# A filter layer's passages through memory dealt anew: rows kept on the chip for two groups instead of four, GpSimd's subtracts ahead of its sends, direct rows from group 10 on, the fourth inverse tile asked for sooner

## The chip, the cores and the metric

The kernel runs on one core of a Trainium2 chip. The metric is the device time of one execution in microseconds (us), the median of several runs; here three runs of the kernel before gave 1383.17, 1384.69 and 1389.86 us. Lower is better. The profile comes from one more execution, taken by the hardware profiler.

Engines are called PE (TensorE matmul), DVE (VectorE), ACT (ScalarE), POOL (GpSimd) and SP (SyncE, which here only issues DMAs). ACT and POOL can issue DMAs too. "SPq" and the like in the profile are the time in which an engine's instruction stream issues DMAs.

## What is computed

Four layers follow one another on x of 2048 rows by 576 columns: attention, filter, attention, filter, each with a layernorm ahead and a residual added. The change touches the filter alone:

```python
def _B_ref(x, w_r, w_i):
    X = rfft2(x, axes=(-2, -1))
    W = w_r + 1j * w_i
    X = X * W
    return irfft2(X, s=(S, D), axes=(-2, -1))      # S = 2048, D = 576
...
x = x + _A_ref(_layernorm(x), A_wqkv, A_wo)        # 32 heads, causal window of 256
x = x + _B_ref(_layernorm(x), B_w_r, B_w_i)
x = x + _A_ref(_layernorm(x), A_wqkv, A_wo)
x = x + _B_ref(_layernorm(x), B_w_r, B_w_i)
```

## The kernel before, in words

**The filter as matmuls.** The transform along the 2048 rows is split as 128 x 16. Sixteen row groups n2 = 0..15 (each 128 rows, 16 apart) each get a transform of length 128 (`f3`, the `pz` matmuls at L289, then `f4`, L296 to L335); that is the forward stage. Sixteen frequency groups g = 0..15 then each take 8 of the 128 results of every n2, 16 x 8 = 128 rows together, and get the transform of length 16, the weights W and the way back (`g0`, `g1m` with the `p` matmuls L476 and L478, `g2` with the `pq` matmuls L497): the middle stage. Sixteen row groups n2 again close with the inverse transform of length 128 (`ly` L551, `i1` with `pi` L560, `i2`, `i3` with `po` L251) and the transform along the columns. In the first filter layer the column transform stands ahead of the row transform (`f1`, `f2`); in the second layer it has been folded into the attention layer's output, so that its forward stage is shorter.

**Two transposes go through memory.** Between the stages the data has to be regrouped: 8 partitions of each of 16 tiles make one tile of 128 partitions. A forward tile `ye` (128 partitions x 580 floats, 290 KB) is written whole to a DRAM tile `yd[0]` (L326); a middle group g is read back from there (L464, two groups per load, 580 KB; the first such load is split into two of 290 KB). The same happens after the middle stage with tiles `ze`/`eo` and `yd[1]` (stores L534), which the inverse stage reads back one n2 at a time (L554).

**Direct rows.** A transpose that ends with "last tile written, then read back" would leave the next stage waiting, so a few tiles that are needed first are also filled directly, chip memory to chip memory, 8 partitions at a time (18.1 KB each). Forward: from n2 = FD = 11 on, every `ye` sends its 8 partitions of groups 0 and 1 (first layer) or 0 to 3 (second layer) by rows (L321) into the middle stage's tiles; what n2 < 11 contributes comes by a bulk load from `yd[0]` (L335, 88 rows of two groups each; one such load in the first layer, two in the second). Middle to inverse: from g = FG = 11 on, every tile sends its 8 partitions of n2 = 0, 1, 2 by rows (L504) into three inverse tiles; bulk loads (L525) bring groups 0 to 7 at g = 10 and 8 to 10 at g = 13.

**Who sends.** The last `ye` tiles are dealt to three engines, for each issue takes its engine about 0.5 to 0.65 us. Second layer: n2 up to 12 and 15 by SP, n2 = 13 by POOL, n2 = 14 by ACT. First layer: n2 = 14 by POOL, all else by SP. In the second layer n2 = 12, 13, 14 have half of `f4`'s arithmetic on POOL (`P.tensor_sub`, L303; ACT's copy of the matmul's result is L293), and n2 = 15 has both halves on DVE (L309, L310).

**Order and waits.** Nothing here is scheduled by a tool: each engine runs its instructions in the order in which the code emits them (`pipe` and the written-out lists call the functions above), and a waiting instruction holds up all behind it on the same engine. DMAs that SP and ACT issue share eight completion semaphores, called DMAHW0 to DMAHW7 and here lanes, handed out in turn over both in an order fixed when the program is built, in which ACT's DMAs stand among SP's. A DMA waits until the one before it on its lane has landed. POOL's DMAs have eight lanes of their own, DMASW0 to DMASW7. So at most eight SP and ACT DMAs are in flight, and an SP DMA can be held by an ACT DMA that has not even been issued.

**Fill-ins.** At the end of the second layer's forward stage 34 matmuls without use (`warm(34)`, L341) keep PE going while the last rows travel, and 36 ahead of its inverse stage. In the first layer useful matmuls (`wo`, L251) stand at these places.

**Residual rows.** `ld` (L164) brings x back for the inverse stage, from g = 11 and 13 on; `i1` adds to it (L562) and the first layer writes it out (L564).

The line that deals the last tiles is the one that names cannot say:

```python
eng = nc.sync if n2 < NT - 3 or n2 == NT - 1 else P if first is (n2 == NT - 2) else nc.sync if first else nc.scalar
```

## Time and profile before

| what | value |
|---|---|
| median of three runs | 1384.69 us (1383.17 to 1389.86) |
| the profiled execution's own time | 1384.23 us |
| its span (first to last instruction) | 1382.3 us |
| granted PE clock, mean | 0.996 |
| PE busy | 1341.2 us, 97% of the span |
| DVE, ACT, POOL busy | 65%, 57%, 47% |
| second layer: forward stage's last `pz`, first `p`, first `pq` | 1259.1, 1272.43, 1278.18 us |
| first layer: first `p`, first `pq` | 604.43, 608.61 us |
| first `pi`: first layer, second layer | 649.30, 1319.14 us |

How to read the views. The *timeline* prints start, duration, engine and line, operation, tile written <- tile read, shape, count, and in square brackets the idle time ahead with what ended it. In a row of SPq, POOL DMA or ACTq the duration is that of the issue, with waits between the joined issues; landing comes later. The *waits* view gives, for an engine's line, the total of its waits, how many, and the longest. The *chain* follows the work that ended last, back from the end, each piece with start and duration; a piece "DMA" is a transfer from issue to landing. The *windows* view has, for each stretch, its length, each engine's busy time in the order PE, PE weight load, DVE, ACT, POOL, then the granted clock (PEclk), the share of the DMA engines' time, and GB/s.

### The profile page before, as it was taken

The page shows a single profiled execution, that of the slowest core. Times are in us where ns is not written, and L with a number is a line of the kernel's source. Part 1 is how long each engine was busy: PE and PEld are TensorE (multiplying, and loading weights), DVE is VectorE, ACT ScalarE, POOL GpSimd, SP SyncE. Part 2 cuts the span into 40 slices and gives each one's busy share as a digit, 9 for nine tenths or more (in the row PEclk, how much of TensorE's full clock was granted, in tenths as well). Part 3 has the DMA queues.
Part 4 walks back from the last instruction along what each step waited for, and adds up shares of the span by engine and source line. Part 5 has one row for each costly group of instructions (what it writes and reads, how often), then busy time and mean ns, then how long its engine had stood idle before and what let it go on. Part 6 is the DMA issues. An engine that isn't in the chain of part 4 may idle for free.

```text
span 1382.3 us, 33597 instructions
## 1 busy us (share of the span) xinstructions
PE 1341.2 (97%) x11356; PEld 998.3 (72%) x11356; DVE 892.7 (65%) x3046; ACT 786.9 (57%) x1978; POOL 646.4 (47%) x1152
## 2 busy tenths in 40 slices
PE   9999999999999999999999999999999999997998
PEld 8985666666665699975899965666666655996588
DVE  5417777877778266566663157787777783563845
ACT  5522777777778544443355316677777778562223
POOL 2257554555547433476221394455545457111821
PEclk9999999999999999999999999999999999999999
DMA  6756665655556457678863467556554565597874
GB/s 202 210 164 185 204 187 174 184 164 164 150 147 181 109 168 238 214 241 272 262 211 73 125 195 220 162 170 165 167 155 143 155 173 153 163 375 216 268 230 159
DMA packets 202478, 259.09 MB, mean 187 GB/s; under 512 B 104589, under 2 KB 109965, under 8 KB 201797
## 3 DMA queue, kind: packets, MB, share of 16 engines
q1 hardware_dynamic: 191573, 235.70, 56.8%
q10 hardware_dynamic: 7856, 15.33, 3.2%
q0 software_dynamic: 2880, 5.93, 1.6%
q8 instruction: 91, 1.49, 0.5%
q14 instruction: 78, 0.64, 0.1%
HBM read 155.98 MB, written 101.01 MB: 186 GB/s over the span
## 4 chain that ended last, share of the span: by engine, by line
PE 81%; POOL 4%; DMA 4%; ACT 4%; DVE 3%; issue 3%; SPq 1%; ACTq 0%; DVEq 0%; POOLq 0%
PE pj L1079 15%; PE S L1136 12%; PE U L1193 11%; PE vps L972 8%; PE ops L767 7%; PE E L1173 5%; PE po L251 4%; PE p L476 2%; PE pf L251 2%; PE tpo L1207 2%; PE pi L560 2%; PE pq L497 2%; ACT P L1174 2%; POOL qs L1227 2%; POOL ks L1226 2%
## 5 line engine op out<-in xcount | busy, mean ns | idle before, releaser
L1138 DVE CUSTOM_DVE_ANT_0 jk<-S,mask 128x384 bf16<-128x384 f32 (+2 forms) x1024 | 490.6, 529 | 112.9 <-PE E L1173 59.3
L1174 ACT ACTIVATE P<-E 128x384 f32<-128x384 f32 (+2 forms) x1024 | 409.5, 476 | 122.9 <-PE E L1173 101.6
L1176 POOL TENSOR_SCALAR_AFFINE_SELECT P<-P 128x512 f32<-128x512 f32 x256 | 163.2, 638 | 280.1 <-ACT P L1174 259.8
L1136 PE MATMUL S<-ks,qs 63*128 63x384 f32 (+2 forms) x1024 | 269.1, 371 | 0.6 <-DVE m L1138 0.4
L1173 PE MATMUL E<-qs,ks 64*128 64x384 f32 (+2 forms) x1024 | 222.4, 372 | 3.5 <-ACT P L1174 1.9
L1136 PEld LDWEIGHTS S<-ks,qs 63*128 63x128 f32 x1024 | 140.6, 185 | 105.3 <-DVE m L1138 72.3
L1193 PE MATMUL U<-P,vq 128*19 128x128 f32 (+1 forms) x3840 | 187.8, 328 | 1.0 <-ACT us L1198 1.0
L1079 PE MATMUL pj<-xh,wqh 128*128 128x512 f32 x360 | 156.1, 434 | 1.4 <-DVE sg L1094 1.0
L1193 PEld LDWEIGHTS U<-P,vq 128*19 128x19 f32 x3840 | 95.6, 98 | 77.5 <-issue 21.8
L1179 POOL TENSOR_SCALAR_AFFINE_SELECT P<-P 128x512 f32<-128x512 f32 x224 | 143.0, 638 | 0.0
L1079 PE MATMUL pj<-xh,wql 128*128 128x512 f32 x360 | 125.8, 423 | 2.4 <-POOL wql L657 2.4
L1173 PEld LDWEIGHTS E<-qs,ks 64*128 64x128 f32 x1024 | 114.3, 185 | 18.2 <-ACT P L1174 8.2
L1079 PE MATMUL pj<-xl,wqh 128*128 128x512 f32 x288 | 122.0, 424 | 0.0
L767 PE MATMUL ops<-oroom 128*128 128x290 f32 (+1 forms) x812 | 115.4, 298 | 0.2
L767 PEld LDWEIGHTS ops<-oroom 128*128 128x128 f32 x812 | 110.3, 189 | 0.7 <-DVE ofree L790 0.7
L1079 PEld LDWEIGHTS pj<-xh,wqh 128*128 128x128 f32 x360 | 67.8, 188 | 32.1 <-issue 10.6
L1094 DVE TENSOR_TENSOR sg<-pj,sg 128x512 fp32r<-128x512 f32 x72 | 49.5, 687 | 56.2 <-ACT sg L1091 56.2
L1138 DVE DVE_READ_ACCUMULATOR2_ANT m<- 128x1 f32 x1024 | 85.0, 83 | 0.0
L1091 ACT CAST sg<-pj 128x512 fp32r<-128x512 f32 x72 | 42.2, 586 | 73.0 <-PE pj L1079 63.1
L1079 PEld LDWEIGHTS pj<-xh,wql 128*128 128x128 f32 x360 | 64.8, 190 | 23.5 <-issue 10.7
L243 ACT CAST et<-tp 128x512 fp32r<-128x512 f32 x53 | 31.2, 589 | 74.1 <-PE tp L239 71.9
L972 PE MATMUL vps<-wvh,xh 128*128 128x288 f32 x320 | 71.4, 304 | 0.1
(225 smaller groups left out, 2304.5 us busy)
## 6 DMA issues: line engine op xcount, KB each, us to landing
qk_d<-sg SPq DMA_DIRECT2D x56, 512.0 KB
qs<-qk_d SPq DMA_DIRECT2D x384, 72.0 KB
ks<-qk_d SPq DMA_DIRECT2D x348, 72.0 KB
v_d<-vt SPq DMA_DIRECT2D x32, 304.0 KB
vq<-v_d SPq DMA_DIRECT2D x16, 608.0 KB
wt<-in_w SPq DMA_DIRECT2D x16, 580.0 KB
ofree<-x SPq DMA_DIRECT2D x16, 580.0 KB
x<-ofree SPq DMA_DIRECT2D x32, 290.0 KB
```

The lines of the kernel that those rows point to most:

```text
L251: T.matmul(ps[:, c, 0:NF], tail[r] if si == 4 else hl_(si), dcs[b // 2][r, b % 2], start=mi == si == 0, stop=si == 4)
L767: self.nc.tensor.matmul(self.ps[u][n][:, 0:self.n], x, self.w[p][:, (2 * wk + n) * self.n:(2 * wk + n + 1) * self.n], start=first and i == ...
L972: T.matmul(ps[:, n, 0:288], xT(xk, c), w[:, wk, n * 288:(n + 1) * 288], start=i == 0, stop=i == len(ks) - 1)
L1079: T.matmul(box["ps"].rearrange("r (n p) -> r n p", n=NT) if second else box["ps"], w[:, wk], x, start=s == 0, stop=s == len(ks) - 1)
L1094: V.tensor_sub(rest[:, 1], by, rest[:, 0].bitcast(F32))
L1136: T.matmul(ps[:, 0:N], q[b:b + 63, pair, i * 128:i * 128 + 128], k[b:b + 63, pair, lo:hi], start=True, stop=True)
L1138: V.tensor_tensor_reduce(out=jk[:, 0:N], in0=ps[:, 0:N], in1=mask[:, 384 - N:384], scale=1.0, scalar=-3e38, op0=ALU.add, op1=ALU.max, accu ...
L1173: T.matmul(ps[:, 0:nq], k[b:b + 64, pair, j * 128:j * 128 + 128], q[b:b + 64, pair, j * 128:j * 128 + nq], start=True, stop=True)
L1174: A.activation(p[:, hl_, 0:nq], ps[:, 0:nq], AF.Exp, scale=SC)
L1176: P.affine_select(out=p[:, :, 0:128], in_=p[:, :, 0:128], pattern=[[0, 4], [1, 128]], compare_op=ALU.is_ge, fill=0.0, base=0, channel_mult ...
L1179: P.affine_select(out=p[:, :, 256:384], in_=p[:, :, 256:384], pattern=[[0, 4], [-1, 128]], compare_op=ALU.is_gt, fill=0.0, base=0, channel ...
L1193: T.matmul(U[32 * h:32 * h + 19, (q0 % 4) * 128:(q0 % 4) * 128 + 128 * (q1 - q0)], vts[n][:, j, h], pt[n, j][:, h, (q0 - j) * 128:(q1 - j) ...
```

## The change

Four things change in the filter layer, in both filter layers unless said otherwise. Line numbers after the change differ; the row send is then L316, the store of a whole `ye` L319, the bulk load L313, the load of groups L474, the rows of the second passage L514, their bulk loads L541, the stores L546, the loads of inverse tiles L569.

1. **Forward rows for groups 0 and 1 only.** The second layer's groups 2 and 3 come back from DRAM like the others; the split load is that of g = 2 in both layers. The one bulk load is issued ahead of n2 = 11's rows.
2. **Second layer, n2 = 13, 14, 15.** POOL first makes its subtracts for 12, 13 and 14; all sends follow after the arithmetic of n2 = 15: rows of 13 by POOL, row 14 for group 0 by SP and for group 1 by POOL, rows of 15 by SP, then the stores: 13 by POOL, 15 by SP, 14 by POOL. ACT sends nothing here any more.
3. **Direct rows of the second passage from g = 10 on** (FG = 10). Bulk loads: groups 0 to 7 at g = 9, ahead of that group's own store, and groups 8 and 9 at g = 11. SP sends the rows to n2 = 0, to n2 = 1 up to g = 12, and one to n2 = 2; ACT those of g = 13 and 15 to n2 = 1; POOL that of g = 14 to n2 = 1, then the store of g = 14, then the other rows to n2 = 2. The held store of g = 13 comes ahead of POOL's last two rows. `ld` is called at g = 10 and 12.
4. **The fourth inverse tile** (n2 = 3), which has no direct rows, is asked for at the start of the inverse stage instead of three steps later.

```diff
@@ -137,7 +137,7 @@
 
     yd = [dram.tile([16, 16, 8, 2 * NF], F32, name=f"yd{j}") for j in range(2)]
     OPEN = *range(2, 17, 2), 17
-    FD, FG, SH = 11, 11, 192
+    FD, FG, SH = 11, 10, 192
     near, NY = 3, 3 if first else 4
     with ExitStack() as stack:
         banks, inner = ExitStack(), ExitStack()
@@ -304,35 +304,45 @@
             else:
                 both = ip.tile([128, 2, NF], F32, tag="both", name=f"half{n2}", bufs=2)
                 A.copy(both[:, 0], pz[:, 1, 0:NF])
-                if not first and n2 == NT - 1:
-                    hs[n2 - 1]["send"]()
                 V.tensor_add(ye[:, 0], pz[:, 0, 0:NF], both[:, 0])
                 V.tensor_sub(ye[:, 1], pz[:, 0, 0:NF], both[:, 0])
             yef = ye.rearrange("p j f -> p (j f)")
             pre(n2)
-            wide = 1 if first else 2
             if n2 == FD:
-                for k in range(wide):
-                    y_tile(k)
-            eng = nc.sync if n2 < NT - 3 or n2 == NT - 1 else P if first is (n2 == NT - 2) else nc.sync if first else nc.scalar
-
-            def rows(lo, hi):
-                for g in range(lo, hi):
-                    eng.dma_start(ys[g][8 * n2:8 * n2 + 8].rearrange("p c f -> p (c f)"), yef[8 * g:8 * g + 8])
-
-            def send():
-                if n2 >= FD:
-                    rows(0, 2 if n2 == NT - 1 else 2 * wide)
+                y_tile(0)
+                nc.sync.dma_start(pairs[0].rearrange("p (a f) -> p a f", a=2)[0:8 * FD], yd[0][0:2, 0:FD].rearrange("a n i f -> (n i) a f"))
+
+            def row(eng, g):
+                eng.dma_start(ys[g][8 * n2:8 * n2 + 8].rearrange("p c f -> p (c f)"), yef[8 * g:8 * g + 8])
+
+            def whole(eng):
                 eng.dma_start(yd[0][:, n2], yef)
-                if n2 == NT - 1:
-                    rows(2, 2 * wide)
-            if eng is nc.scalar:
-                h["send"] = send
+
+            if n2 < FD:
+                whole(nc.sync)
+            elif first:
+                e = P if n2 == NT - 2 else nc.sync
+                for g in range(2):
+                    row(e, g)
+                whole(e)
+            elif n2 < NT - 3:
+                for g in range(2):
+                    row(nc.sync, g)
+                whole(nc.sync)
             else:
-                send()
-            if n2 == FD:
-                for k in range(wide):
-                    nc.sync.dma_start(pairs[k].rearrange("p (a f) -> p a f", a=2)[0:8 * FD], yd[0][2 * k:2 * k + 2, 0:FD].rearrange("a n i f -> (n i) a f"))
+                h["rows"] = [lambda e, g=g: row(e, g) for g in range(2)]
+                h["whole"] = whole
+            if not first and n2 == NT - 1:
+                a, b, c = hs[n2 - 2:]
+                a["rows"][0](P)
+                a["rows"][1](P)
+                b["rows"][0](nc.sync)
+                b["rows"][1](P)
+                c["rows"][0](nc.sync)
+                c["rows"][1](nc.sync)
+                a["whole"](P)
+                c["whole"](nc.sync)
+                b["whole"](P)
 
         def warm(n):
 
@@ -460,7 +470,7 @@
         def g0(g, h):
             if g % 2 == 0 and g not in ys:
                 y = y_tile(g // 2).rearrange("p a c f -> p a (c f)")
-                for a in ((0, 1), (1, 2)) if g == (2 if first else 4) else ((0, 2),):
+                for a in ((0, 1), (1, 2)) if g == 2 else ((0, 2),):
                     nc.sync.dma_start(y[:, a[0]:a[1]], yd[0][g + a[0]:g + a[1]].rearrange("a n i f -> (n i) a f"))
             h["y"] = ys[g]
 
@@ -476,8 +486,8 @@
                     T.matmul(ps[64 * j:64 * j + 64, c, 0:NF], fc[:, g, j, c], h["y"][:, j], start=True, stop=g > 0)
                     if g == 0:
                         T.matmul(ps[64 * j:64 * j + 64, c, 0:NF], fc[:, 16, j, c], h["y"][:, 1 - j], start=False, stop=True)
-            if g in (11, 13):
-                ld(g - 11)
+            if g in (10, 12):
+                ld(g - 10)
             w = wt[g]
             p1 = tws[g % 2]
             p2 = wp.tile([128, 2, NF], F32, tag="tc", name=f"p2_{g}", bufs=3)
@@ -509,26 +519,28 @@
                 V.tensor_sub(ye[:, 1], pq[:, 0, 0:NF], both[:, 1])
                 if first:
                     w1(3)
-                for n2 in range(2):
-                    rows(nc.sync, n2, 15)
+                rows(nc.sync, 0, 15)
+                for k in (13, 15):
+                    rows(nc.scalar, 1, k)
+                held.pop()()
                 for k in (14, 15):
                     rows(P, 2, k)
-                held.pop()()
             else:
                 A.copy(both, pq[:, :, 0:NF])
                 P.tensor_sub(ye[:, 1, 0:SH], both[:, 0, 0:SH], both[:, 1, 0:SH])
                 V.tensor_add(ye[:, 0], pq[:, 0, 0:NF], both[:, 1])
                 V.tensor_sub(ye[:, 1, SH:NF], pq[:, 0, SH:NF], both[:, 1, SH:NF])
-            if g in (FG - 1, FG + 2):
+            if FG <= g < 15:
+                for n2 in range(1 if g > 12 else 2):
+                    rows(nc.sync, n2, g)
+            if g == 12:
+                rows(nc.sync, 2, FG)
+            if g in (FG - 1, FG + 1):
                 lo, hi = (0, 8) if g < FG else (8, FG)
                 for n2 in range(near):
                     nc.sync.dma_start(yis[n2][8 * lo:8 * hi].rearrange("p c f -> p (c f)"), yd[1][n2, lo:hi].rearrange("g i f -> (g i) f"))
             if g == 14:
-                for k in range(FG, 14):
-                    rows(P, 2, k)
-            if FG <= g < 15:
-                for n2 in range(2):
-                    rows(P if g == 14 and n2 else nc.sync, n2, g)
+                rows(P, 1, 14)
 
             def store():
                 (P if g == 14 else nc.scalar if g < 13 and (g < 8 or g % 2 == 0) else nc.sync).dma_start(yd[1][:, g], yef)
@@ -536,6 +548,9 @@
                 held.append(store)
             else:
                 store()
+            if g == 14:
+                for k in range(FG + 1, 14):
+                    rows(P, 2, k)
 
         zs, held = {}, []
         pipe(16, [(10, g2), (7, g1m), (2, gw), (0, g0)])
@@ -549,9 +564,9 @@
             next(nxt)
 
         def ly(n2, h):
-            y = h["y"] = yis[n2 % 4]
-            if n2 >= near:
-                nc.sync.dma_start(y.rearrange("p c f -> p (c f)"), yd[1][n2].rearrange("g i f -> (g i) f"))
+            h["y"] = yis[n2 % 4]
+            for k in (near,) if n2 == 0 else (n2,) if n2 > near else ():
+                nc.sync.dma_start(yis[k % 4].rearrange("p c f -> p (c f)"), yd[1][k].rearrange("g i f -> (g i) f"))
 
         def i1(n2, h):
             pi = pp.tile([128, 2, 512], F32, tag="mm", name=f"pi{n2}", bufs=3)
```

**On SP, end of the second layer's forward stage, before.** The names: `ye_19786` is n2 = 12, `ye_19825` is n2 = 15; `ofree` is the memory of the middle stage's tiles; the brackets hold the semaphores waited for.

```order
L321 DMA ofree<-ye_19786 8x580 [waits DMAHW7_49,DVE_49,Pool_49]
L321 DMA ofree<-ye_19786 8x580 [waits DMAHW1_49]
L321 DMA ofree<-ye_19786 8x580 [waits DMAHW2_49]
L321 DMA ofree<-ye_19786 8x580 [waits DMAHW3_49]
L326 DMA yd_18874<-ye_19786 16x8x580 [waits DMAHW4_49]
L321 DMA ofree<-ye_19825 8x580 [waits DMAHW5_49,DVE_49]
L321 DMA ofree<-ye_19825 8x580 [waits DMAHW6_49]
L326 DMA yd_18874<-ye_19825 16x8x580 [waits DMAHW7_49]
L321 DMA ofree<-ye_19825 8x580 [waits DMAHW0_49]
L321 DMA ofree<-ye_19825 8x580 [waits DMAHW1_49]
L464 DMA ofree<-yd_18874 128x580 [waits DMAHW4_49,DMAHW2_49,DMAHW7_49,DMASW2_49,Activation_49]
```

On ACT at the same place, where `ye_19813` is n2 = 14:

```order
L321 DMA ofree<-ye_19813 8x580 [waits DMAHW1_49,DMAHW6_49,DVE_49,Pool_49]
L321 DMA ofree<-ye_19813 8x580 [waits DMAHW3_49,DMAHW2_49]
L321 DMA ofree<-ye_19813 8x580 [waits DMAHW4_49]
L321 DMA ofree<-ye_19813 8x580 [waits DMAHW6_49]
L326 DMA yd_18874<-ye_19813 16x8x580 [waits DMAHW0_49]
```

**After,** on SP, from n2 = 12 (`ye_19786`) over n2 = 14 (`ye_19806`) and 15 (`ye_19818`) to the first load of the middle stage:

```order
L316 DMA ofree<-ye_19786 8x580 [waits DVE_49,Pool_49]
L316 DMA ofree<-ye_19786 8x580 [waits DMAHW4_49]
L319 DMA yd_18877<-ye_19786 16x8x580 [waits DMAHW5_49]
L316 DMA ofree<-ye_19806 8x580 [waits DMAHW6_49,DVE_49,Pool_49]
L316 DMA ofree<-ye_19818 8x580 [waits DMAHW7_49,DVE_49]
L316 DMA ofree<-ye_19818 8x580 [waits DMAHW0_49]
L319 DMA yd_18877<-ye_19818 16x8x580 [waits DMAHW1_49]
L474 DMA ofree<-yd_18877 128x580 [waits DMAHW1_49,DMAHW2_49,DMASW2_49,DMAHW5_49,DMASW1_49,PE_49]
L474 DMA ofree<-yd_18877 128x580 [waits DMAHW3_49,PE_49]
```

Before, SP's second row of n2 = 12 and ACT's first row of n2 = 14 have the same lane, DMAHW1, in which ACT's comes first; ACT's five took lanes 1, 3, 4, 6 and 0. After, ACT's are gone, SP has two rows of n2 = 12 and one of n2 = 14, and the store of n2 = 15 stands behind both its rows; the loads of group 2 now stand where those of group 4 stood.

**On POOL at the same place.** Before (`ye_19803` is n2 = 13, `ye_19813` is n2 = 14):

```order
L303 TENSOR_TENSOR ye_19786<-half_19774 128x290 [waits DMAHW0_49,DMAHW3_49,DVE_49,Activation_49]
L303 TENSOR_TENSOR ye_19803<-half_19804 128x290 [waits DMAHW4_49,DVE_49,Activation_49]
L321 DMA ofree<-ye_19803 8x580 [waits DMAHW2_49,DMAHW6_49,DVE_49,Pool_49]
L321 DMA ofree<-ye_19803 8x580 [waits DMAHW7_49,DMAHW2_49]
L321 DMA ofree<-ye_19803 8x580 [waits PE_49] x2
L326 DMA yd_18874<-ye_19803 16x8x580
L303 TENSOR_TENSOR ye_19813<-half_19814 128x290 [waits DMAHW0_49,Activation_49]
```

After (`ye_19801` is n2 = 13, `ye_19806` is n2 = 14):

```order
L303 TENSOR_TENSOR ye_19786<-half_19774 128x290 [waits DMAHW3_49,DMAHW6_49,DVE_49,Activation_49]
L303 TENSOR_TENSOR ye_19801<-half_19802 128x290 [waits DMAHW7_49,DVE_49,Activation_49]
L303 TENSOR_TENSOR ye_19806<-half_19807 128x290 [waits DMAHW3_49,DMAHW1_49,Activation_49]
L316 DMA ofree<-ye_19801 8x580 [waits DMAHW1_49,DMAHW5_49,DVE_49,Pool_49]
L316 DMA ofree<-ye_19801 8x580 [waits DMAHW5_49,DMAHW2_49]
L316 DMA ofree<-ye_19806 8x580 [waits DVE_49,Pool_49]
L319 DMA yd_18877<-ye_19801 16x8x580
L319 DMA yd_18877<-ye_19806 16x8x580
```

The subtract of n2 = 14 moves from behind the five sends of n2 = 13 to ahead of all sends; two rows of n2 = 13 fall away, one row and the store of n2 = 14 are new.

**On SP, start of the first layer's inverse stage.** Before, from the last store of the middle stage (`ze_10158`, g = 15) on:

```order
L534 DMA yd_8102<-ze_10158 16x8x580 [waits DMAHW4_49]
L164 DMA ofree<-x_59 128x1160 [waits DMAHW5_49,PE_49]
L564 DMA x_60<-ofree 128x580 [waits DMAHW6_49,DVE_49]
L164 DMA ofree<-x_59 128x1160 [waits DMAHW7_49,PE_49]
L554 DMA ofree<-yd_8102 128x580 [waits DMAHW3_49,DMAHW4_49,DMAHW0_49,DMASW1_49]
```

After (`ze_10160` is g = 15):

```order
L546 DMA yd_8102<-ze_10160 16x8x580 [waits DMAHW7_49]
L569 DMA ofree<-yd_8102 128x580 [waits DMAHW6_49,DMAHW7_49,DMAHW0_49,DMASW6_49]
L164 DMA ofree<-x_59 128x1160 [waits DMAHW1_49,PE_49]
L579 DMA x_60<-ofree 128x580 [waits DMAHW2_49,DVE_49]
L164 DMA ofree<-x_59 128x1160 [waits DMAHW3_49,PE_49]
```

The load of inverse tile n2 = 3 moves up past two loads of x and one store of x.

## The prediction

> **What bounds the kernel now.** I read the page first: what share PE has, and whether the chain that ended last runs over PE.
>
> ```profile
> PE 1341.2 (97%) x11356; PEld 998.3 (72%) x11356; DVE 892.7 (65%) x3046; ACT 786.9 (57%) x1978; POOL 646.4 (47%) x1152
> PE 81%; POOL 4%; DMA 4%; ACT 4%; DVE 3%; issue 3%; SPq 1%; ACTq 0%; DVEq 0%; POOLq 0%
> ```
>
> PE is busy for 1341.2 of 1382.3 us. The change leaves PE's matmuls as they are, so it can win only PE's idle time, or lose by adding some. The waits view of PE says where the filter layers leave it idle.
>
> ```profile
> PE p L476 <- DMA ofree<-ye: 8.7, 1, 8.7
> PE pi L560 <- issue: 1.9, 1, 1.9
> PE pi L560 <- DMA ofree<-ze: 1.8, 1, 1.8
> PE pi L560 <- DMA ofree<-yd: 1.1, 1, 1.1
> ```
>
> One wait of 8.7 us for rows and three of 1 to 2 us in the inverse stages are all that the change can reach: 13.5 us. The timeline says which layer the long one is in, and why it is there.
>
> ```profile
> 1258.28 0.80 POOL L303 TENSOR_TENSOR ye<-half 128x290 f32<-128x290 f32 x1 [1.15 <-ACT half L293]
> 1258.96 4.80 PE L341 MATMUL warm<-dc 128*128 128x290 f32 x34
> 1259.27 9.63 SPq L321 DMA_DIRECT2D ofree<-ye  x4
> 1259.49 2.09 POOL L321 DMA_DIRECT2D ofree<-ye  x4 [0.41 <-DVE ye L302]
> 1260.01 0.45 DVE L310 TENSOR_TENSOR ye<-pz,half 128x290 f32<-128x290 f32 x1
> 1261.57 0.55 POOL L326 DMA_DIRECT2D yd<-ye  x1
> 1262.14 0.72 POOL L303 TENSOR_TENSOR ye<-half 128x290 f32<-128x290 f32 x1
> 1262.88 2.78 ACTq L321 DMA_DIRECT2D ofree<-ye  x4
> 1269.62 1.30 SPq L321 DMA_DIRECT2D ofree<-ye  x2
> 1272.43 1.24 PE L476 MATMUL p<-ofree,fc 128*64 128x290 f32 x4 [8.66 <-DMA ofree<-ye]
> ```
>
> It is the second layer. SP needs 9.63 us for the four rows of n2 = 12, of which the waits view of SP puts 7.0 on one landing:
>
> ```profile
> SPq L321 <- DMA ofree<-ye: 7.0, 1, 7.0
> 1262.88 4.01 DMA ofree<-ye
> 1269.62 2.47 DMA ofree<-ye
> 1278.18 2.15 PE pq L497 x8
> ```
>
> The order rows of SP and ACT name it: SP's second row of n2 = 12 has lane 1 behind ACT's first row of n2 = 14. In the chain (the last three rows) that row is issued at 1262.88 and lands 4.01 later, at 1266.89; SP goes on there. ACT's row could not go sooner, since POOL subtracted for n2 = 14 at 1262.14 only, behind five sends of 1259.49 to 1262.12. So the data of n2 = 15, complete at 1260.46 (DVE, 1260.01 + 0.45), is sent at 1269.62, its second row lands for the `p` of group 0 at 1272.43, and the first `pq` starts at 1278.18. A second price hangs on that idle time, in the windows view:
>
> ```profile
> 1264.00:1272.40 8.40, 0.00 (x0) 0.01 (x1) 0.00 (x0) 0.00 (x0) 0.00 (x0) 0.79 0.44 113
> 1272.40:1276.20 3.80, 3.77 (x18) 2.31 (x20) 0.00 (x0) 0.00 (x0) 0.00 (x0) 0.56 0.55 149
> 1276.20:1312.00 35.80, 35.80 (x249) 19.16 (x245) 30.24 (x60) 9.59 (x15) 28.57 (x46) 1.00 0.86 277
> ```
>
> After 8.4 us of idleness the granted clock is 0.56, and group 0 takes 3.80 us. From 1276.2 PE is full to 1312.
>
> **Second layer, forward tail.** ACT's five DMAs leave the lanes, and POOL subtracts before it sends. The subtract of n2 = 14 ends at about 1259.8 (1258.28 + 0.80 + 0.72). The rows of n2 = 12 are two instead of four, 0.65 each. Three rows remain on SP after them: n2 = 14 to group 0 at 1259.8, n2 = 15 at 1260.5 and 1261.15 (not before 1260.46), then the store of n2 = 15 at 1261.8. POOL issues three rows of about 0.52 (2.09 for four) from 1259.8, then its stores at 1261.35 and 1261.9. With 2.47 to landing, the row of n2 = 15 is there at 1263.6. `warm(34)` ends at 1263.76, so group 0 starts at about **1263.8** and the wait of 8.7 us is gone.
>
> What is late next is group 2: it now comes through memory. Its load waits for the stores of n2 = 13, 14, 15. The nearest rows for these landings, the first two from the DMA issues (second and first layer's tail: KB, us to landing), the rest from the first layer, which already runs that way:
>
> ```profile
> yd<-ye POOLq DMA_DIRECT2D x1, 290.0 KB, 5.1
> yd<-ye POOLq DMA_DIRECT2D x1, 290.0 KB, 3.0
> 603.70 8.60 SPq L464 DMA_DIRECT2D ofree<-yd  x6
> 604.50 0.65 PE p L476 x4
> 606.66 1.96 PE p L476 x16
> 608.61 2.15 PE pq L497 x8
> 652.76 6.75 DMA ofree<-yd
> ```
>
> There the load of group 2 was asked at 603.7 and PE went through groups 1 and 2 from 606.66 to 608.61 without a gap, so the load (290 KB) took at most 3.9 us (group 2's half of 1.96 us began at about 607.6); the worst load of 290 KB in a filter layer is the 6.75. At a full clock group 0 takes 2.16 us (604.50 to 606.66) and group 1 0.98. Here group 0 ends at about 1266.0 and group 1 at 1266.95. POOL's last store, issued at 1261.9, lands 3.0 to 5.1 later: 1264.9 to 1267.0. The load takes 3.9 (I keep up to 6.75 for the range). With 3.0 and 3.9 group 2 starts at 1268.8 after an idle 1.85 us, and `pq` at about **1269.5**, with 2.75 as the price of a load in the faster case down to 1268.6. Before it was 1278.18: a gain of **8.6**. Bounds: 5.1 and 6.75 put group 2 at 1273.75 and `pq` at 1274.7, a gain of 3.5; a free landing of all (`pq` as soon as the product of group 0 allows, 608.61 − 604.50 = 4.1 after 1263.8, or 1268.0) gives 10.2.
>
> Two things can hold this. The row of n2 = 14 has the lane of the bulk load, issued now at about 1252.3, when the store of n2 = 10 has landed; even with 7.06 us, the largest piece of the chain that is a load (in the fence below), it lands at 1259.4, ahead of 1259.8: nothing. And later loads are asked as much sooner as group 2 is, so they keep their lead over PE's 2.3 us a group: nothing.
>
> **The Trainium skill speaks against the dealing.** "DMA: Bandwidth & Descriptors", section "Issuing engines are not separate DMA queues", says that DMAs started from several engines run on the same 16 DMA engines, and that spreading them saves only issue time. By that rule alone the three stores and the load are 1.16 MB one after another, whoever sends them; at the 277 GB/s of the full window this is 4.2 us from 1261.4, an estimate that puts group 2 at 1265.6, ahead of PE, so the rule would take nothing from this step. The trace agrees with the rule in kind (POOL's store took 5.1 us beside other transfers, 3.0 without), but what cost 7 us was a lane, not a DMA engine.
>
> **Second layer, inverse start.**
>
> ```profile
> 1305.42 7.06 DMA ofree<-x
> 1312.28 5.06 PE L341 MATMUL warm<-dc 128*128 128x290 f32 x36
> 1313.25 0.45 DVE L509 TENSOR_TENSOR ze<-pq,both 128x290 f32<-128x290 f32 x1
> 1315.49 3.52 DMA ofree<-ze
> 1319.14 2.20 PE L560 MATMUL pi<-ofree,ga 128*128 128x290 f32 x8 [1.80 <-DMA ofree<-ze]
> ```
>
> The last tile is complete at 1313.70, but SP sends its row to n2 = 0 at 1315.49, behind rows of g = 13 and 14. After, SP has one row each of g = 13, 14 and 15 here instead of two, two, of which one by POOL, and two: it issues the last at 1314.1 to 1314.8, and it lands by 1316.6 (with 2.47) to 1318.3 (with 3.52). `warm(36)` ends at 1317.34. `pi` starts at 1317.4 to 1318.3 instead of 1319.14: 0.8 to 1.75, I take **1.5**. ACT's two rows to n2 = 1 follow its last copy, with nothing behind them that is wanted soon; POOL's rows to n2 = 2 come behind two stores now, about 1 us later, but `pi` of n2 = 2 comes over 3 us after the first (the chain has it at 1322.56). The `ld` calls, one group sooner, fall into a stretch in which PE is full: nothing, unless loads then come late (bounded by the 1.0 below).
>
> **First layer, inverse start.**
>
> ```profile
> 648.41 0.54 SPq L164 DMA_DIRECT2D ofree<-x  x1
> 649.30 2.19 PE L560 MATMUL pi<-ofree,ga 128*128 128x290 f32 x8 [1.90 <-issue]
> 649.38 0.59 ACT L243 CAST et<-tp 128x512 fp32r<-128x512 f32 x1 [1.96 <-DMA ofree<-ze]
> 652.76 0.34 SPq L554 DMA_DIRECT2D ofree<-yd  x1
> 659.55 1.25 PE L560 MATMUL pi<-ofree,ga 128*128 128x290 f32 x4 [1.10 <-DMA ofree<-yd]
> ```
>
> The fourth tile's load moves from behind two loads and a store of x to the place of 648.41, where it must wait for the last stores (some 2 us), so 650 to 651, 2 or more before 652.76. Its 6.75 may grow by the transfers that it now runs beside, but it needs to come only 1.1 earlier: the wait of **1.1** goes. The loads of x that it passes are each 0.35 to 0.54 later. The first `pi` could start sooner, as in the second layer, but ACT's cast at 649.38 waits for the same landings and the `wo` matmuls behind the first `pi` wait for it; I give this nothing, with 0 to 1.6 for the two together, and −1.0 if POOL's later rows to n2 = 2 hold it.
>
> The forward tail of the first layer keeps its two rows per tile, and `wo` matmuls cover it until `p` at 604.50: the bulk load's new place costs nothing while they do, at most the few tenths by which its rows follow later.
>
> **Sum,** against the profiled execution's own 1384.23 us (span 1382.3, 1.9 outside; 0.46 under the median of the three runs): 8.6 + 1.5 + 1.1 = 11.2, so **1373.0**.
>
> **Rivals.**
>
> *Congested landings.* Store and load of group 2 take 5.1 and 5 to 6.75 us: `pq` starts at 1272.9 to 1274.7. PE then idles 5 to 6.8 us between groups 1 and 2. A stage gain of 3.5 to 5.3 and 2.6 from the rest give **1376.3 to 1378.1**. For it: POOL's store did take 5.1 here. Against: two bulk loads stood ahead of it, of which one is left, sent 3.6 us sooner.
>
> *The inverse starts give nothing* (1.5 and 1.1 fall away, because the rows of g = 15 land behind stores as at 1315.49, or because ACT's rows share lanes with SP's): **1374.5 to 1375.6**.
>
> *The trip through memory becomes the bound, on the slower side.* If store and load each take 7.06, as the load of x did, group 2 comes at 1261.9 + 14.1 = 1276.0. PE has then been idle for 9 us, longer than the 8.4 after which group 0 took 3.80 us for 2.16. Groups 2, 3 and the first two `pq` at a clock of 0.56 lose about 2 us; the first full `pq` is 1.5 us later than before, and with the inverse starts unchanged: **1385.7**. It decides from group 2 later than 1276.2 on. Against: no store of 290 KB took more than 5.1. "TensorE: Matmul & The Clock Gate" of the Trainium skill, Part 1, puts the drop to half clock after an idle window of about 3.4 us; the trace agrees in kind (0.79 over the idle window, 0.56 behind it), and by it the congested rival would pay 1 to 2 us too and come to 1377 to 1380.
>
> *It doesn't free SP:* another lane or POOL's sends hold the rows of n2 = 15 as long as before. Then only the 2.6 of the rest remain: **1381.6**. The order rows speak against it.
>
> **Chances.** Forecast 0.61 (1371.3 to 1374.5), inverse starts give nothing 0.13, congested landings 0.18, SP not freed 0.04, slower side 0.04. The range 1370.5 to 1378.5 leaves out the last two and a little at the ends. 0.5%, about what a measurement of this kernel can tell from no change, is 6.9 us: faster is below 1377.8. Forecast, inverse case and some 0.11 of the congested one lie there: 0.84; within, 0.13; slower beyond 0.5% is a part of the slower side: 0.03.
>
> **What would show it.** Right: no SP wait of 7 us at the rows of n2 = 12; both rows of n2 = 15 issued by 1262; `p` within 0.3 us of the end of `warm(34)`, and group 0 in 2.2 us; a PE wait of 1 to 3 us at the load of group 2; `pq` 8 to 9 us sooner; `pi` of the second layer waiting under 1 us; no wait at the first layer's fourth `pi`. Wrong: PE waiting 5 us or more for group 2, a granted clock below 1 behind it, or a landing of n2 = 14's store that ends later than 1267.

## The result and the profile after

The changed kernel takes 1387.64 us (median of 22 runs, 1383.39 to 1392.41) against 1383.61 us before (22 runs): ratio **1.0028**, 95% interval 1.0019 to 1.0038. It is slower by about 4 us; forecast were 1373.0 us and a range up to 1378.5. The profiled execution took 1388.67 us with a span of 1387.0 (before: 1384.23 and 1382.3), so the two profiles differ as the medians do, by 4.7 and 4.0 us.

PE's busy time, in a line of the page, has grown by 4.6 us with the same number of matmuls; the mean granted clock of the profiled execution is 0.993 instead of 0.996.

```profile
PE 1345.8 (97%) x11356; PEld 1003.0 (72%) x11356; DVE 892.3 (64%) x3046; ACT 786.5 (57%) x1978; POOL 644.9 (46%) x1152
```

PE's waits in the changed kernel (total, times, longest), in the same view as before:

```profile
PE wo L251 <- DVE et L245: 5.4, 2, 3.0
PE pi L575 <- DMA ofree<-ze: 3.9, 1, 3.9
...
PE wo L251 <- ACT et L243: 2.1, 1, 2.1
PE p L486 <- DMA ofree<-ye: 2.1, 1, 2.1
```

The wait of 8.7 us for rows is down to 2.1; forecast was none. In front of `wo` matmuls, which belong to the first layer's inverse start, PE waits 7.5 us, and the second layer's first `pi` waits 3.9 instead of 1.8 us. Before, the view had for `wo` only

```profile
PE wo L251 <- ACT et L243: 0.7, 1, 0.7
```

To see which stretch gives and which takes, three of them are followed through all kernels below. **A** runs from the start of `warm(34)` to the start of the second `pq` (second layer, forward to middle). **B** runs in the first layer, and **C** in the second, from the start of the last 24 `pq` matmuls (groups 13 to 15) to the start of `pi` of n2 = 4, where the inverse stage has found its pace. Each is the difference of two starts of PE rows in the timeline. For B of the changed kernel these are:

```profile
638.43 3.27 PE L507 MATMUL pq<-uv,m 64*128 64x290 f32 x24
651.27 3.13 PE L575 MATMUL pi<-ofree,ga 128*128 128x290 f32 x8
662.19 1.81 PE L575 MATMUL pi<-ofree,ga 128*128 128x290 f32 x4
666.66 1.14 PE L575 MATMUL pi<-ofree,ga 128*128 128x290 f32 x4
670.18 1.14 PE L575 MATMUL pi<-ofree,ga 128*128 128x290 f32 x4
```

The first `pi` row holds n2 = 0 and 1, the others one n2 each, so B is 670.18 − 638.43 = 31.75 us. Before it was 663.17 − 639.51 = 23.66.

| stretch | before | changed | difference | forecast |
|---|---|---|---|---|
| A, second layer's forward tail | 22.43 | 15.80 | −6.6 | −8.6 |
| B, first layer's inverse start | 23.66 | 31.75 | **+8.1** | −1.1 |
| C, second layer's inverse start | 21.68 | 24.55 | +2.9 | −1.5 |
| sum | | | +4.3 | −11.2 |

The sum accounts for 4.3 of the 4.7 us between the spans. So the gain came, if smaller, and the first layer's inverse start gave it all back. The timeline of the changed kernel there:

```profile
641.64 0.53 ACTq L546 DMA_DIRECT2D yd<-eo  x1
642.26 1.19 ACT L529 COPY both<-pq 128x580 f32<-128x580 f32 x2 [4.14 <-PE pq L507]
642.82 1.99 SPq L514 DMA_DIRECT2D ofree<-eo  x3
646.50 0.53 POOL L530 TENSOR_TENSOR eo<-both 128x192 f32<-128x192 f32 x1 [2.99 <-DMA ofree<-eo]
647.77 0.62 SPq L514 DMA_DIRECT2D ofree<-ze  x1
655.67 0.59 ACT L243 CAST et<-tp 128x512 fp32r<-128x512 f32 x1 [4.79 <-DMA ofree<-eo]
657.37 2.78 PE L251 MATMUL wo<-dc,et 128*128 128x290 f32 x10 [2.97 <-DVE et L245]
```

Two things stand out. ACT stood 4.14 us in front of its copies, behind its store of group 12. And GpSimd's subtract for group 14 (646.50) waited 2.99 us for a *direct row* to land. Group 14 writes into an `eo` tile, of which the first layer has two in turn here (`eos[2 + g // 2 % 2]`): group 14's is that of group 10. Direct rows from group 10 on read that tile, and the last of them, to n2 = 2, is sent by SP at group 12, as the third in the row at 642.82. Before, group 10 had no direct rows. Everything of group 14 comes later by that: SP's last row goes out at 647.77, 9.3 us after the last 24 `pq` began (before: 645.70 and 646.38, so 6.2 and 6.9 us), and a cast that reuses the tiles' memory waits for the last rows until 655.67. The windows view shows what idleness then costs (clock in the third column from the right):

```profile
645.90:648.38 2.48, 0.05 (x1) 0.00 (x1) 1.96 (x5) 0.00 (x0) 1.35 (x3) 0.62 0.08 15
648.38:651.20 2.82, 2.82 (x12) 2.80 (x13) 0.00 (x0) 0.64 (x1) 2.76 (x6) 0.50 0.66 162
651.20:654.40 3.20, 3.20 (x10) 2.04 (x8) 0.00 (x0) 0.00 (x0) 0.00 (x0) 0.67 0.68 181
654.40:657.40 3.00, 0.03 (x1) 0.04 (x1) 0.78 (x2) 0.86 (x2) 0.00 (x0) 0.89 0.42 107
657.40:662.00 4.60, 4.60 (x20) 4.58 (x21) 1.37 (x4) 0.64 (x1) 1.37 (x6) 0.50 0.96 295
```

In 16 us PE works 10.6 at a clock of 0.50 to 0.67.

### The profile page after: what moved, and what is told of

It is laid out like the page before. It is cut to its first block, busy times and chain, and to the rows that moved or that the text cites. A ratio compares the mean times of both kernels' runs of the same rounds, so it can differ in the third digit from the quotient of the medians.

```text
span 1387.0 us, 33579 instructions
## 1 busy us (share of the span) xinstructions
PE 1345.8 (97%) x11356; PEld 1003.0 (72%) x11356; DVE 892.3 (64%) x3046; ACT 786.5 (57%) x1978; POOL 644.9 (46%) x1152
## 4 chain that ended last, share of the span: by engine, by line
PE 81%; DMA 6%; ACT 4%; POOL 3%; DVE 3%; issue 2%; SPq 1%; ACTq 0%; DVEq 0%; POOLq 0%
PE pj L1094 17%; PE S L1151 11%; PE U L1208 10%; PE vps L987 8%; PE ops L782 7%; PE E L1188 5%; PE po L251 4%; PE pf L251 2%; PE p L486 2%; PE pi L575 2%; PE tpo L1222 2%; PE pq L507 2%; ACT P L1189 2%; PE pz L289 1%; DMA qs<-mt 1%
## 5 line engine op out<-in xcount | busy, mean ns | idle before, releaser
L1094 PEld LDWEIGHTS pj<-xh,wqh 128*128 128x128 f32 x360 | 67.7, 188 | 32.6 <-issue 10.5
```

The lines of the kernel that those rows point to most:

```text
L1094: T.matmul(box["ps"].rearrange("r (n p) -> r n p", n=NT) if second else box["ps"], w[:, wk], x, start=s == 0, stop=s == len(ks) - 1)
```

## The experiments

My theory after this reading: part 3 of the change (direct rows from group 10 on) loses what part 2 wins, by the buffer of group 14. The first rival: the lanes, held by the x loads that part 3 asks one group sooner (ACT's 4.14 us). Each kernel was run with 6 to 12 timed runs beside the kernel before; ratios are to the kernel before, with 95% intervals, and "the changed kernel" is always the one of the result.

A, B and C come from one profiled execution of each kernel. How far they scatter can be seen where the code of a stretch is the same. A is 15.66 to 18.40 us in the nine kernels that have the changed forward stage as it is (changed, e1, e4, e5, e6, e8, e9, e12, e15); B is 22.61 to 24.41 and C 20.52 to 22.65 in the four that have the inverse start of e8 (e8, e10, e13, e14). So a difference of under 2 us in B or C, or under 3 in A, shows nothing by itself.

### The parts alone: e1_forward, e2_passage, e3_tile

e1 is the kernel before with parts 1 and 2, e2 with part 3, e3 with part 4; the diffs are those pieces of the change.

> The kernel before with parts 1 and 2 of the change alone (forward rows for two groups, GpSimd's subtracts ahead of its sends, no ACT sends). My theory: this part keeps what the trace of the changed kernel shows of it (the stretch from the last pz to the first pq of the second layer was 6.7 us shorter), and the loss comes from part 3. So 6 to 7 us faster than before, ratio 0.995 to 0.996. Rival: the forward tail gives less by itself, since part of the 6.7 us is only the later start of that stretch (other transfers have drained): 2 to 4 us, ratio 0.997 to 0.999.

> The kernel before with part 3 alone (direct rows from group 10 on, bulk loads at 9 and 11, rows dealt anew, x asked one group sooner). My theory: the whole loss is here, 8 us in the first layer's inverse start and 2 to 3 in the second's, so 9 to 11 us slower than before, ratio 1.0065 to 1.008. Rival: the loss needs part 4 beside it (the fourth tile's load waits for the last stores on SP, and everything of SP stands behind it): then part 3 alone costs 3 us or less.

> The kernel before with part 4 alone (fourth inverse tile asked for ahead of the x loads). Forecast of the prediction: the 1.1 us wait at the first layer's fourth pi goes, ratio 0.999. Rival: the load waits for the last stores and holds the x loads and x stores behind it on SP by 2 to 4 us; pi of the fourth tile then gains nothing, and the time is the same or up to 2 us longer, ratio 1.000 to 1.0015.

| kernel | median us | ratio | A | B | C |
|---|---|---|---|---|---|
| before (profile) | | 1 | 22.43 | 23.66 | 21.68 |
| e1_forward | 1376.17 | 0.9961 (0.9946 to 0.9976) | 16.71 | 24.02 | 21.28 |
| e2_passage | 1395.39 | 1.0095 (1.0079 to 1.0111) | 22.60 | 34.46 | 23.97 |
| e3_tile | 1381.93 | 0.9994 (0.998 to 1.0009) | 22.69 | 24.35 | 21.11 |

Parts 1 and 2 give 5 to 6 us by themselves; part 3 alone costs 13 us, more than the 9 to 11 expected, and needs no part 4; part 4 makes no difference that these runs can tell. The three ratios multiplied give 1.005, more than the change's 1.0028: in company part 3 costs some 3 us less than alone, which these runs don't explain.

### The x loads: e4_ld, e9_xpool

```diff
-            if g in (10, 12):
-                ld(g - 10)
+            if g in (11, 13):
+                ld(g - 11)
```

> The changed kernel with the two x loads back at groups 11 and 13. Theory of the lane: the 580 KB load of x, asked one group sooner, takes 7.3 us and has the lane that ACT's store of group 12 needs; ACT stands 4 us in front of the copies of groups 13 to 15. With the loads back ACT's wait goes and 4 to 7 us of the loss in the two inverse starts, so 1380 to 1383, ratio to before 0.996 to 0.999. Theory of the buffer: the tile of group 14 waits in the first layer for the direct rows of group 10 (3.0 us on POOL), and the rows behind GpSimd's store are late whatever the lanes do: then the gain is under 2 us, ratio to before 1.001 to 1.003.

e9 leaves the loads where the change put them, on another queue:

```diff
-                nc.sync.dma_start(x, xfv[:, n2:n2 + 2])
+                (P if n2 < 4 else nc.sync).dma_start(x, xfv[:, n2:n2 + 2])
```

> The changed kernel with the first two loads of x (580 KB each, ahead of the inverse stage) issued by GpSimd, so that they use no lane of SP and ACT. Theory of the lane: ACT's store of group 12 (4 us in both layers) and SP's rows no longer wait for such a load to land, the second layer's inverse start loses its 2.9 us against before and the first layer's some 1 to 2: ratio to before 0.999 to 1.0005, if GpSimd's own issue costs no more than 1 us. Theory of the buffer: the first layer's loss stays, and only what the second layer's lanes cost is won: 1.0005 to 1.002.

e4: 1386.51 us, 1.0033 (1.002 to 1.0047); B 30.99, C 23.46. e9: 1386.55 us, 1.0033 (1.002 to 1.0045); B 29.94, C 23.47. Both lie above what was expected of the lanes, and a little above the ranges given for the buffer. ACT's wait for a lane is gone in e4, yet B is only 0.8 shorter. GpSimd's waits in that stretch of e4 say why:

```profile
POOL eo L530 <- issue: 4.6, 1, 4.6
```

The subtract of group 14 now waits 4.6 instead of 3.0 us (the view finds no last releaser; it starts at 644.99, after the SP row of group 10, the last of three issued from 641.30 to 643.29). A wait was taken away and the next one on the path filled its place. The lanes of the x loads fall as the explanation of B. C is 1.1 us shorter in both, which is within the scatter and shows nothing for the lanes there.

### The buffer: e5_early, e6_pool, e8_fg11

e5 sends the one late row of group 10 two groups sooner:

```diff
-            if g == 12:
+            if g == FG:
                 rows(nc.sync, 2, FG)
```

> The changed kernel, with the one row of group 10 for inverse tile n2 = 2 sent by SP at group 10 instead of group 12. Theory of the buffer: in the first layer group 14 writes into the tile of group 10, and GpSimd's subtract for it waits 3.0 us for this row to land (4.6 us with x loaded later). With the row sent early that wait goes, and the first layer's inverse start gains 3 to 5 us: ratio to before 0.999 to 1.001. Rival (rows behind the stores): GpSimd then starts sooner but its rows to n2 = 2 still land behind the three last stores, ACT's cast waits for them as before: gain under 1.5 us, ratio to before 1.002 to 1.004.

e6 puts GpSimd's rows of groups 11 to 13 ahead of its store of group 14 again:

```diff
             if g == 14:
                 rows(P, 1, 14)
+                for k in range(FG + 1, 14):
+                    rows(P, 2, k)
...
-            if g == 14:
-                for k in range(FG + 1, 14):
-                    rows(P, 2, k)
```

> The changed kernel, with GpSimd's rows of groups 11 to 13 to n2 = 2 ahead of its store of group 14, as they stood before the change. Theory of the buffer: GpSimd is late because of the subtract of group 14, the order behind it is worth under 1 us: ratio to before 1.002 to 1.004. Rival: the rows land 5 us after their issue because they come behind GpSimd's and SP's stores; ahead of the first of them they land some 2 us sooner, and the cast and pi with them: ratio to before 1.000 to 1.0015.

e8 keeps the whole change but for one number:

```diff
-    FD, FG, SH = 11, 10, 192
+    FD, FG, SH = 11, 11, 192
```

> The changed kernel with direct rows from group 11 on again, so with bulk loads at groups 10 and 12 (0 to 7, 8 to 10) and the new dealing of rows. Group 10 then has no direct rows, so nothing of the first layer's group 14 waits for one. Theory of the buffer: ratio to before 0.998 to 1.000, the gain of the forward tail less what the second layer's lanes take. Rival (the new dealing itself is slow): 1.002 to 1.004, as the changed kernel.

| kernel | median us | ratio | A | B | C |
|---|---|---|---|---|---|
| changed (profile) | | 1.0028 (1.0019 to 1.0038) | 15.80 | 31.75 | 24.55 |
| e5_early | 1382.39 | 1.0004 (0.9989 to 1.0019) | 17.14 | 26.94 | 23.64 |
| e6_pool | 1386.08 | 1.0031 (1.0019 to 1.0043) | 17.24 | 31.78 | 22.26 |
| e8_fg11 | 1377.19 | 0.997 (0.9957 to 0.9983) | 17.15 | 22.90 | 20.87 |

The theory of the buffer holds. One row sent sooner shortens B by 4.8 us (the ratio falls by 0.0024, 3.3 us). The lanes shift with it (ACT stands 2.86 instead of 4.14 us in front of its copies), but e4 and e9, where ACT's wait for the x load is gone, shorten B by 0.8 and 1.8 only. With direct rows from group 11 on, B and C are no longer than before the change, and the time lies below the range expected; e8 also has the bulk loads one group later, so it shows what the number 10 costs as a whole and not the buffer alone. GpSimd's order behind the subtract is worth nothing in time. GpSimd's waits for the subtract of group 14 in the changed kernel and in e8:

```profile
POOL eo L530 <- DMA ofree<-eo: 3.0, 1, 3.0
```

```profile
POOL eo L530 <- POOL ze L530: 0.2, 1, 0.2
```

### What group 10's rows cost besides: e12_ld, e15_clock

e5 still has B 3.3 and C 2.0 us above before. e12 is e5 with the x loads at groups 11 and 13 as in e4.

> The changed kernel with the row of group 10 to n2 = 2 sent at group 10 and the x loads back at groups 11 and 13. The early row alone left 3.3 us of the first layer's loss and 2 of the second's. If the lanes held by the 580 KB loads of x account for the rest (SP's second bulk load waited for one to land), it goes now: ratio to before 0.997 to 0.9985. If it is the number of small transfers that direct rows from group 10 on put into the tail, nothing more is won: 1.000 to 1.001.

e15 is e5 with useless matmuls through the waits of both inverse starts:

```diff
         if first:
             w2(3)
+            warm(24)
         else:
-            warm(36)
+            warm(56)
```

> The changed kernel with the row of group 10 to n2 = 2 sent at group 10 (1.0004 of before), and matmuls without use ahead of both inverse starts: 24 in the first layer, 56 instead of 36 in the second. PE waited 4.7 and 2.9 us there and ran the next 4.1 us at a granted clock of about 0.5. If the clock makes up what is left of the loss, each inverse start is 1.5 to 2 us shorter: ratio to before 0.997 to 0.9985. If late transfers alone bound it, the useless matmuls take the place of idleness: 1.000 to 1.001.

e12: 1380.96 us, 0.9982 (0.997 to 0.9994), B 26.72, C 23.63. e15: 1378.99 us, 0.9982 (0.9965 to 0.9999), B 24.39, C 23.00. For e12 the two measures disagree: the time is 0.2% under e5's, with intervals that overlap, but B and C have e5's length, so I take nothing from it on the lanes. In e12 SP sent its last row 7.4 us after the last 24 `pq` began, in e8 6.6 us after. For e15 the stretches say what it is. In e5 (two windows around its first `pi`):

```profile
645.60:650.37 4.77, 0.04 (x2) 0.03 (x1) 0.00 (x0) 1.14 (x3) 0.87 (x2) 0.70 0.62 176
650.37:654.50 4.13, 4.13 (x9) 2.96 (x10) 1.51 (x3) 0.37 (x2) 0.69 (x3) 0.52 0.61 207
```

PE waits 4.77 us and then runs at 0.52. With PE kept busy the first `pi` starts hardly sooner (11.9 us after the last 24 `pq` began, 12.4 in e5), but it runs at full clock, and B is 2.6 us shorter. So of e5's rest in B some 2.5 us go with the halved clock, though the intervals of the two times overlap a little. In C the matmuls win 0.6. What stays, 0.7 in B and 1.3 in C, is within the scatter; that later landings make it is not shown.

### The forward tail: e11_order, e10_bulk, e13_warm, e14_best

e11 is the kernel *before* with only GpSimd's order changed (the sends of n2 = 13 kept until the subtract of n2 = 14 has been issued).

```diff
             if eng is nc.scalar:
+                hs[n2 - 1]["send"]()
                 h["send"] = send
+            elif not first and n2 == NT - 3:
+                h["send"] = send
             else:
```

> The kernel before with one thing changed: GpSimd's subtract of n2 = 14 ahead of its five sends of n2 = 13; ACT still sends n2 = 14 and groups 0 to 3 still come by rows. Theory of the lane in the forward tail: ACT's first row goes 3 us sooner, SP's second row of n2 = 12 with it, p 2.5 to 3.5 us sooner: ratio to before 0.9975 to 0.9985. Rival: the ring of eight lanes is full of slow landings there anyway (the rows landed at 1265.7 to 1266.9 behind two bulk loads) and p comes under 1 us sooner: 0.9993 to 1.000.

Measured: 1381.93 us, 0.9995 (0.9983 to 1.0008), A 21.89: the 3 us did not come. The waits of PE and of SP in the tail of e11:

```profile
PE p L479 <- DMA ofree<-ye: 7.8, 1, 7.8
```

```profile
SPq L338 <- DMA ofree<-ye: 6.5, 2, 5.0
```

ACT's first row does go sooner, but the lanes have been handed out in another turn, and now SP's second bulk load (L338), ahead of the rows of n2 = 12, stands 5.0 us for a row. By the times it is one of ACT's, of which the first went out at 1256.18; the view does not name it. And a second hold ends last, as the chain of e11 shows:

```profile
1259.06 6.42 DMA yd<-ye
...
1265.54 2.04 DMA ofree<-ye
...
1267.82 1.24 PE p L479 x4
```

ACT's store of n2 = 14, issued at 1259.06, took 6.42 us, and SP's first row of n2 = 15 went out when it had landed. The hold has moved within SP's list, not gone. In e1 ACT sends nothing in between, and SP's rows of n2 = 12 take 1.34 us for two.

The last three build on e8. e10 moves the forward bulk load back behind the rows and the store of n2 = 11:

```diff
             if n2 == FD:
                 y_tile(0)
-                nc.sync.dma_start(pairs[0]...)
...
+            if n2 == FD:
+                nc.sync.dma_start(pairs[0]...)
             if not first and n2 == NT - 1:
```

> The kernel with direct rows from group 11 (the last one but with FG = 11), and besides the forward bulk load back behind the rows and the store of n2 = 11. What it tests: the bulk load ahead of that store delays its landing, and the tile of n2 = 15 is the buffer of n2 = 11 (DVE waited 1.35 and 1.9 us for it in two runs, 0.5 in others). If that is what made the rows of n2 = 15 late, p starts at the end of the useless matmuls in every run and the time is 0 to 1.5 us shorter than with the bulk load first: ratio to before 0.9955 to 0.997. If the bulk load itself then lands too late for group 0, p waits 1 us or more: 0.997 to 0.999.

e13 fills PE's wait for group 2 in the second layer; e14 is e10 and e13 together.

```diff
         def g1m(g, h):
+            if g == 2 and not first:
+                warm(16)
             ps = pp.tile([128, 2, 512], F32, tag="mm", name=f"p2_{g}", bufs=3)
```

> The kernel with direct rows from group 11, with 16 matmuls without use ahead of p of group 2 in the second layer, where PE waited 3.15 us for the load and then ran groups 2 and 3 at a granted clock of 0.64 for 4.7 us. If the clock is what these 4.7 us cost, the matmuls keep it at 1.00 and win 1 to 1.7 us: ratio to before 0.9955 to 0.9965. If the load's landing is what bounds (pq of group 0 has to wait for nothing else), the matmuls take the place of idleness and win nothing: 0.997.

> The two helpful edits together: direct rows from group 11, the forward bulk load behind the store of n2 = 11, and 16 matmuls without use ahead of p of group 2. The stretch from the first useless matmul to the second pq was 17.2 us with the first edit alone and 15.7 with the second alone, which still had 1.0 us of waiting for the rows of n2 = 15. Together: 15 to 15.7 us, ratio to before 0.9945 to 0.9955. If the two work on the same wait, no better than the better of them: 0.995 to 0.996.

| kernel | median us | ratio | A | B | C |
|---|---|---|---|---|---|
| e10_bulk | 1378.85 | 0.9963 (0.9949 to 0.9977) | 17.17 | 22.61 | 20.52 |
| e13_warm | 1376.62 | 0.9949 (0.9931 to 0.9968) | 15.69 | 24.41 | 22.62 |
| e14_best | 1375.53 | 0.9957 (0.9942 to 0.9973) | 15.37 | 22.84 | 22.65 |

In e13's profile A is 1.5 us shorter than in e8's, since `p` and `pq` of the next groups keep their clock there. That the useless matmuls do this every time is not shown: e15 has none at this place and an A of 15.66, and the intervals of the times of e8 and e13 overlap. e8's two windows around PE's wait for group 2, and then e13's over the matmuls and what follows:

```profile
1265.55:1268.70 3.15, 0.00 (x0) 0.03 (x1) 1.82 (x3) 0.00 (x0) 2.60 (x4) 1.00 0.53 174
1268.70:1273.40 4.70, 4.70 (x16) 2.75 (x16) 1.43 (x2) 0.00 (x0) 1.37 (x2) 0.64 0.97 337
```

```profile
1268.35:1270.80 2.45, 2.45 (x20) 2.29 (x20) 1.89 (x3) 0.00 (x0) 2.45 (x4) 1.00 0.89 306
1270.80:1275.50 4.70, 4.70 (x28) 2.65 (x30) 2.15 (x5) 0.64 (x1) 2.11 (x4) 1.00 0.89 309
```

The two edits together have the shortest A of all, by 0.3 us, which is within the scatter. e1, e8, e10, e13 and e14 are all faster than the kernel before, by 0.3 to 0.5%, and so than the changed one; their intervals overlap: which of them is best stays open. The bulk load's place (e10) makes no difference in time that these runs can tell; in its profile the wait for the buffer of n2 = 11 is gone.

## Why the prediction was wrong, point by point

**What bounds the kernel: right.** Lanes shared with ACT held SP for 7 us. e1, where ACT sends nothing, ends that, and in e11, where ACT still sends but sooner, its DMAs in SP's turn hold SP at two other places.

**Second layer, forward tail: mechanism right, size at least 2 us too large.** In the changed kernel:

```profile
1267.09 4.70 PE L351 MATMUL warm<-dc 128*128 128x290 f32 x34
1268.18 3.23 SPq L316 DMA_DIRECT2D ofree<-ye  x3
1269.26 0.46 DVE L307 TENSOR_TENSOR ye<-pz,half 128x290 f32<-128x290 f32 x1 [1.86 <-DMA yd<-ye]
1271.46 0.58 SPq L319 DMA_DIRECT2D yd<-ye  x1
1273.85 0.72 PE L486 MATMUL p<-ofree,fc 128*64 128x290 f32 x4 [2.07 <-DMA ofree<-ye]
1279.61 2.22 PE L507 MATMUL pq<-uv,m 128*128 128x290 f32 x8
```

Forecast was that the data of n2 = 15 is complete when the arithmetic allows. DVE waited 1.86 us more, because the tile of n2 = 15 is the buffer of n2 = 11 (four in turn), whose store, now behind the bulk load, had not landed. So `p` waited 2.07 us where no wait was forecast, and `pq` came 12.5 us after the start of `warm(34)`, not the 10.5 that 1269.5 meant. In the nine profiles of this forward stage A is 4.0 to 6.8 us shorter than before, never 8.6. From the first `p` to `pq` it took 5.76 us, and 5.7 were forecast, but that is luck: there was no wait for group 2's load; instead group 0 ran at a clock of 0.60 and took 3.25 us instead of 2.16.

```profile
1271.78:1273.85 2.07, 0.01 (x1) 0.03 (x1) 0.00 (x0) 0.00 (x0) 0.00 (x0) 1.00 0.84 251
1273.85:1277.10 3.25, 3.25 (x16) 2.04 (x18) 0.00 (x0) 0.00 (x0) 0.00 (x0) 0.60 0.37 97
```

The wait for group 2's load was forecast at 1.85 us; where `p` was on time it was 3.2 to 3.4 us (e5, e8, e12, e15), long enough for the clock to drop in most of them.

**First layer, inverse start: the step that failed.** I credited the fourth tile's earlier load with 1.1 us and bounded the rest by 1 us of loss, "if POOL's later rows to n2 = 2 hold it". The prediction went through part 3 by queues, lanes and landings, and nowhere asked which *buffers* the new rows read. That rows of group 10 hold the tile that group 14 writes is in the code (two `eo` tiles in the first layer, four in the second), not in the trace of before, where nothing waited there. In its place the runs showed that it cost B 4.8 of its 8.1 us (e5), and e8 that all of the loss goes when direct rows start at group 11. The 1.1 us of the fourth tile did not come either: its load, forecast for 650 to 651, went out at 655.18, since it waits for the last stores. With part 4 alone (e3) the wait at the fourth `pi` is gone, but the first `pi` waits 2.38 instead of 1.90 us, and no gain can be told in the time.

**Second layer, inverse start: wrong sign.** I had the last row go out 0.7 to 1.4 us sooner. The chain of the changed kernel:

```profile
1307.39 7.20 DMA ofree<-eo
1314.61 0.60 SPq L546
...
1319.10 3.28 DMA ofree<-ze
```

Group 10's first row was sent at 1307.39 right behind a 580 KB load of x and landed 7.20 us later; its lane held SP's store of group 11 until 1314.61, and all rows of groups 12 to 15 came behind. The last went at 1319.10, 8.5 us after the last 24 `pq` began, where before it was 6.4. I had priced rows at 2.47 to 3.52 us to landing, and the earlier x load at nothing. That load held ACT's store of group 12 as well, and with it the copies of groups 13 to 15:

```profile
1315.10 1.19 ACT L529 COPY both<-pq 128x580 f32<-128x580 f32 x2 [4.84 <-DMA ofree<-x]
1317.32 0.45 DVE L519 TENSOR_TENSOR ze<-pq,both 128x290 f32<-128x290 f32 x1
```

So the last tile was complete at 1317.77, 7.2 us after the last 24 `pq` began (before: 4.6), and its row could not have gone sooner, however free SP was. Which of the two holds costs what is not shown: C is 23.46 us with the x load later (e4), 23.64 with one row of group 10 sooner (e5), 23.63 with both (e12), and back at 20.87 only without group 10's rows (e8).

I followed lanes in the forward tail only; one rival named them here, but priced them at no more than the gain. The trace of before had such a hold at the first layer's inverse start, in its chain:

```profile
635.57 6.51 DMA yd<-eo
...
642.10 0.34 SPq L525
...
646.38 3.00 DMA ofree<-ze
```

ACT's store of group 10 took 6.51 us, and SP's second set of bulk loads, with all rows of groups 13 to 15 behind it, waited for its landing.

**The rivals.** "The inverse starts give nothing" was the nearest, but stopped at zero. The slower side that I priced, group 2's trip through memory, did not occur. What I set against it, that no store of 290 KB took more than 5.1 us, was wrong: the chain above has one of 6.51. Nor do POOL's two stores show that a store is slow beside other transfers: the DMA engines were busy for a share of 0.72 during the one of 3.0 us and of 0.55 during the one of 5.1. And no row shows the 2.75 us that stood for a load in the faster case. Of the 15.7 us between forecast and profiled execution, B makes 9.2, C 4.4, A 2.0; the range held none of the first two, since a step that is thought free gets no bound.

## What to carry to other kernels

A transfer that reads a tile for longer is a longer lease on its buffer: for each added send, find who writes that buffer next, and when, before pricing the send itself. And price the same edit in each layer that uses the code: here one index with two buffers in one layer and four in the other made the same row hold nobody's buffer in one and cost about 5 us in the other.

A wait that goes away is worth only its distance to the next one on the path (e4, e11). And idleness of 2 to 5 us ahead of PE's work is paid twice where the clock drops behind it.

## What the runs showed of the hardware that I had not expected

The granted clock does not follow the length of a wait alone. After 2.07 us the changed kernel ran at 0.60 and after 3.15 us without matmuls e8 ran 4.7 us at 0.64 (both above); e15, at the same place as e8 and after 3.44 us, ran on at 1.00:

```profile
1267.40:1270.84 3.44, 0.02 (x2) 0.04 (x1) 1.84 (x3) 0.00 (x0) 2.62 (x4) 1.00 0.50 161
1270.84:1275.20 4.36, 4.36 (x24) 2.46 (x24) 1.69 (x3) 0.64 (x1) 1.59 (x3) 1.00 0.99 346
```

"TensorE: Matmul & The Clock Gate" of the Trainium skill, Part 1, says that the clock is judged in a free-running window of about 3.4 us. That fits two like waits with unlike ends; that a wait shorter than the window brought the drop does not follow from it, and here the measurement decides. For a forecast it means that a wait of this length has two prices, some 1.5 us apart.

An 18 KB row needed 2.47 us to landing in the forward tail of before and 7.20 us when it was issued 0.6 us behind a 580 KB load; a 290 KB store issued 0.3 us behind such a load, in the changed kernel's first layer, needed 7.23. In both cases the large load ahead seems to set the price of what follows; no run changes that alone.
